# First MLP split into 6 and 10 tiles of features, with every block sum of the second MLP's matrices formed beside the second half and kept in DRAM

## The chip, the cores and the metric

The kernel runs on one core of one Trainium2 chip. The metric is the device time of one execution in microseconds (us); lower is better. Engines are named as the profile names them: PE (TensorE matmuls) and PEld (its weight loads), DVE (VectorE), ACT (ScalarE), POOL (GpSimd), SP (SyncE, which issues the DMAs).

## The reference

Attention over 4 batches, 8 heads, 576 positions and 64 dimensions per head, with a causal mask and a decay bias; then two MLPs over the 2304 tokens of width 512:

```python
x = attn(q, k, v, s)                    # (2304, 512)
h = x @ w_in                            # 512 -> 2048
g = s * relu(h) ** 2 + b
x = g @ w_out                           # 2048 -> 512
h = max(x @ w1, x @ w2, x @ w3)         # 512 -> 768
out = h @ w_fin                         # 768 -> 512
```

The matrices of both MLPs arrive as 64-bit numbers. `w_in` and `w_out` are the first MLP's (inputs `moe_`), `w1`, `w2`, `w3` and `w_fin` the second's (inputs `moe2_`).

## The kernel before

Every MLP product is made from two 32-bit parts of each operand, hi and lo, by three matmuls (`mm3`, lines 252 to 254). A 64-bit matrix is turned into hi and lo on the chip: `weight_steps` (line 266) loads a piece, then runs some nine operations on ACT, DVE and POOL (lines 282 to 297).

The 2048 features of the first MLP are 16 tiles of 128. The first `f_split` = 8 of them (**half A**, matrices `wa_in`, `wa_out`, tiles `g`, `ga`) are worked beside attention: for each of 4 batches and each of 2 parts of its tokens (320 and 256 columns) the products go up to 8 tiles (lines 252 to 254 with `xhi`, `xlo`, `wa_in`), are squared after a relu on DVE and ACT, and come down into 4 tiles of outputs (`ga`, `wa_out`), which wait in DRAM as `y0_d`. Attention itself is 20 jobs, 4 and 4 for the two parts of batch 0 and 12 whole ones; its last product is `px` (line 623). The other 8 tiles (**half B**, `wb_in`, `wb_out`, tiles `gbh`, `gbl`) run after attention and after half A, over 5 groups of tokens (`AT`: two of 384 columns, three of 512). `mlp1` (line 995) records both halves. The matrices of half B are converted during attention in pieces of 256 columns (`side`, line 897; tiles `wb`, `wbs`) and saved in DRAM (`wb_d`), and are loaded when attention's memory is given back (`begin_2`, line 914).

The second MLP's three products use a scheme with 7 products per block of 2 by 2 (Strassen-Winograd), so each matrix is first turned into 7 block sums per half of its rows (a **quad**; `convert_quad`, line 1204; 6 quads in all). Each quad loads four blocks of 128x384 (tiles `wst`, `bl`), runs bit operations on ACT and DVE, and forms hi and lo of seven sums. Three quads (`STAGED`, line 1274) are formed beside the last part of half A, in tiles `sd` that lie where `wb_out` will come, and saved to DRAM (`s_d`); the other three beside half B. The two of `w1` (i = 0) stay in SBUF as `sw`; those of `w2`, `w3` are saved, and loaded piece by piece into 12 slots `sdp` when the third part needs them (`load_s`, line 1371; `weight`, line 1377). `middle_o` (line 922) gives the memory of `sd` to `wb_out`, `middle_2` (line 926) gives half A's memory to half B, and `begin_3y`, `begin_3z`, `begin_3` (lines 941 to 968) give half B's to the second MLP.

The order of the work is not written out by hand. Each step is added with its engines, a cost, a priority, what it needs and which slot of a ring it takes; `Plan.order` (line 96) places all steps one after the other by these costs and so fixes each engine's order for good. Half A's matmuls have the lowest priority on PE and fill what attention leaves. The order on an engine is followed as it stands: an instruction that waits holds up all behind it.

Of the kernel before, what the change touches and what calls it, by code (L numbers as in the profile page):

```python
# [18 lines left out]
P = 128  # L19
# [180 lines left out]
def fused_kernel(ctx, tc, q, k, v, s, w_in, w_out, ms, mb, w1, w2, w3, w_fin, out,  # L200
                 f_split=8):
# [457 lines left out]
    def in_us(fixed, each):  # L659
# [8 lines left out]
                 "ws": 2, "wg": 3, "wx": 1, "wb": 3, "p": 3, "ph": 4, "raw": 2, "hs": 2, "wst": ST2, "bl": 8, "ts": 2, "sp": 12, "s2": 7, "o": 3, "sd": sum(SD), "xs": XS_BUFS, "y0": 3, "g2": 2})  # L668
# [228 lines left out]
    side = pieces(None, NE, NB * P, w_in[:, NA * P:], 512) + pieces(None, NB, DM, w_out[NA * P:, :], 512)  # L897
    for y, piece in enumerate(side):
        for h in range(2):
            z = 2 * y + h  # L900
            t = WB_1 + z * WB_S
            convert("s", z, SidePiece(z, piece.src[piece.c * P:(piece.c + 1) * P, piece.n0 + h * HB:piece.n0 + (h + 1) * HB]), stage_b, [t + d for d in W_AT],
                    [("w", "a", x, 8) for x in WX] + [("av", 2 * NP - 1 - x, g) for x in range(2) for g in jobs[2 * NP - 1].groups], "wb", None, att=True)
            add(("save", z), "SP", (1, 2 * HB), t + 3.5, [("w", "s", z, 8)], save_b, z, att=True)
# [9 lines left out]
    def begin_2():  # L914
# [26 lines left out]
    def begin_3y():  # L941
# [615 lines left out]
```

## Time and profile before

| | |
|---|---|
| time, median of 3 runs | 906.7 us (903.11 to 907.07) |
| the profiled execution's own time | 906.37 us |
| its span, first to last instruction | 904.6 us |
| PE busy | 881.3 us, 97% of the span |
| PEld, DVE, ACT, POOL busy | 89%, 69%, 55%, 37% |
| attention's last product (`px`) | ends at 344.4 us |
| half A's last matmul | 432.5 us |
| mean granted TensorE clock | 0.992 |

The stages follow one another on PE: attention with half A as filler up to 344.4 us, the rest of half A up to 432.5 us, half B, and the second MLP from about 640 us to the end. A matmul's busy time in the profile is longer than the distance at which matmuls follow one another, so distances are read from starts.

### The profile page before, as it was taken

What the parts mean: (1) busy time and instruction counts of PE and PEld (TensorE: products, weight loads), DVE (VectorE), ACT (ScalarE), POOL (GpSimd) and SP (SyncE); (2) the same over time, 40 slices, a digit from 0 to 9 for tenths busy, and PEclk for the clock granted to TensorE, in tenths of its full rate; (3) what the DMA queues carried; (4) which work ended last, traced back from release to release, by engine and by line L of the source; (5) the groups of instructions that cost most, each with busy time, mean ns of one, the idle gap of its engine ahead of it and who ended that gap; (6) DMA issues with size and microseconds to landing.
All of it is one profiled execution on the core that took longest, in us unless ns stands there. A gap on an engine that the chain in (4) does not pass through costs nothing.

```text
span 904.6 us, 16566 instructions
## 1 busy us (share of the span) xinstructions
PE 881.3 (97%) x5598; PEld 804.7 (89%) x5598; DVE 625.8 (69%) x1506; ACT 494.0 (55%) x1241; POOL 334.9 (37%) x359
## 2 busy tenths in 40 slices
PE   7799899999999999999999999999999999999998
PEld 7567798899898899999999888888999899989996
DVE  7799978778778635888349796676666566656660
ACT  4688689999995763455435445254224422532321
POOL 3335447745655322333312333042224422432220
PEclk9899999999999999999999999999999999999999
DMA  7445455675565204686836454438797255715501
GB/s 225 153 136 182 158 171 185 190 231 174 165 217 188 82 21 149 227 282 219 300 126 232 142 180 157 143 107 226 219 286 221 85 163 172 224 71 163 164 24 70
DMA packets 145652, 154.47 MB, mean 171 GB/s; under 512 B 10144, under 2 KB 112288, under 8 KB 145568
## 3 DMA queue, kind: packets, MB, share of 16 engines
q1 hardware_dynamic: 145472, 153.26, 54.2%
q8 instruction: 45, 0.74, 0.3%
q14 instruction: 39, 0.32, 0.1%
q10 hardware_dynamic: 96, 0.15, 0.0%
HBM read 111.36 MB, written 42.01 MB: 170 GB/s over the span
## 4 chain that ended last, share of the span: by engine, by line
PE 62%; DVE 1%; DMA 1%; issue 0%; ACT 0%; SPq 0%; POOL 0%; ACTq 0%; DVEq 0%; POOLq 0%
PE mm L253 20%; PE mm L254 20%; PE mm L252 20%; DMA wst<-in_moe_w_dram 1%; PE px L623 1%; PE pt L604 0%; DVE g L1022 0%; PE ps L546 0%; DVE ya L1084 0%; DVE sd L1153 0%; DVE wst L1180 0%; PE pr L594 0%; ACT bl L1169 0%; DVE bl L1153 0%; DVE wst L1178 0%
## 5 line engine op out<-in xcount | busy, mean ns | idle before, releaser
L1026 ACT ACTIVATE g<-g 128x320 f32<-128x320 f32 (+3 forms) x104 | 51.7, 497 | 93.0 <-DVE g L1022 92.7
L248 POOL TENSOR_TENSOR gbl<-g,gbh 128x512 fp32r<-128x512 f32 (+1 forms) x40 | 50.4, 1261 | 125.6 <-ACT gbh L241 124.7
L563 ACT ACTIVATE pp<-pp,mn 128x192 f32<-128x192 f32 (+4 forms) x160 | 88.6, 558 | 3.6 <-DVE mn L557 3.5
L248 POOL TENSOR_TENSOR ga<-g,ga 128x320 fp32r<-128x320 f32 (+1 forms) x64 | 57.4, 898 | 83.4 <-ACT ga L241 80.7
L248 POOL TENSOR_TENSOR set<-raw,set 64x1152 fp32r<-64x1152 f32 x24 | 64.5, 2687 | 62.7 <-ACT set L480 49.5
L604 PE MATMUL pt<-ident,pp 128*128 128x128 f32 x480 | 78.9, 279 | 7.5 <-ACT pt L241 4.5
L1022 DVE TENSOR_SCALAR g<-mm 128x320 f32<-128x320 f32 (+3 forms) x104 | 54.2, 521 | 44.5 <-PE mm L254 44.0
L252 PE MATMUL mm<-ty,sdp 128*128 128x384 f32 x252 | 84.2, 334 | 0.0
L253 PE MATMUL mm<-ty,sdp 128*128 128x384 f32 x252 | 84.2, 334 | 0.0
L254 PE MATMUL mm<-ty,sdp 128*128 128x384 f32 x252 | 84.2, 334 | 0.0
L252 PE MATMUL mm<-xhi,wa_in 128*128 128x320 f32 (+1 forms) x256 | 79.6, 311 | 1.3 <-DVE ya L1084 1.3
L252 PE MATMUL mm<-ga,wa_out 128*128 128x320 f32 (+2 forms) x256 | 80.3, 314 | 0.1
L254 PE MATMUL mm<-ga,wa_out 128*128 128x320 f32 (+2 forms) x256 | 76.6, 299 | 2.7 <-DVE wa_out L297 2.7
L241 ACT ACTIVATE pt<-pt 128x256 f32<-128x256 f32 (+3 forms) x181 | 72.2, 427 | 11.9 <-PE pt L604 9.0
L253 PE MATMUL mm<-ga,wa_out 128*128 128x320 f32 (+2 forms) x256 | 76.4, 299 | 1.2 <-POOL ga L248 1.2
L253 PE MATMUL mm<-xlo,wa_in 128*128 128x320 f32 (+1 forms) x256 | 75.7, 296 | 0.2 <-POOL xlo L248 0.2
L254 PE MATMUL mm<-xhi,wa_in 128*128 128x320 f32 (+1 forms) x256 | 75.7, 296 | 0.0
L557 DVE CUSTOM_DVE_ANT_0 pp<-late_keys,ps 64x64 f32<-64x64 f32 (+4 forms) x160 | 63.1, 419 | 17.5 <-PE ps L546 10.9
L604 PEld LDWEIGHTS pt<-ident,pp 128*128 128x128 f32 x480 | 56.0, 141 | 16.3 <-ACT pt L241 6.5
L254 PE MATMUL mm<-gbh,wb_out 128*128 128x512 f32 (+2 forms) x160 | 58.9, 368 | 0.0
L252 PE MATMUL mm<-gbh,wb_out 128*128 128x512 f32 (+2 forms) x160 | 58.9, 368 | 0.0
L253 PE MATMUL mm<-gbl,wb_out 128*128 128x512 f32 (+2 forms) x160 | 58.9, 368 | 0.0
(243 smaller groups left out, 2583.6 us busy)
## 6 DMA issues: line engine op xcount, KB each, us to landing
sdp<-s_d SPq DMA_DIRECT2D x126, 256.0 KB, 4.5
wst<-in_moe_w_dram SPq DMA_DIRECT2D x24, 384.0 KB, 5.5
s_d<-sd SPq DMA_DIRECT2D x21, 384.0 KB, 2.5
raw<-in_q_dram SPq DMA_DIRECT2D x24, 288.0 KB, 3.6
raw<-in_k_dram SPq DMA_DIRECT2D x24, 288.0 KB, 3.2
wb_d<-wbs SPq DMA_DIRECT2D x21, 256.0 KB, 2.7
bl<-y_d SPq DMA_DIRECT2D x24, 192.0 KB, 4.4
out_dram<-o SPq DMA_DIRECT2D x18, 256.0 KB, 2.0
```

The lines of the kernel that those rows point to most:

```text
L241: nc.scalar.activation(dst, src, AF.Copy, scale=1.0 if scale is None else scale)
L248: ENGINES[on].tensor_tensor(dst, a, b, op=ALU.subtract)
L252: nc.tensor.matmul(ps, lhs[0], rhs[0], start=first, stop=False)
L253: nc.tensor.matmul(ps, lhs[0], rhs[1], start=False, stop=False)
L254: nc.tensor.matmul(ps, lhs[1], rhs[0], start=False, stop=last)
L557: nc.vector.tensor_tensor_reduce(out=pp[j][i][:n, k0:k1], in0=late_keys[:n, a:a + k1 - k0], in1=ps_.pop((job.n, u, j))[:n, :k1 - k0], scal ...
L563: nc.scalar.activation(p[:n, :w], p[:n, :w], AF.Exp, bias=mns[job.n, j][:n, i:i + 1], scale=-1.0, accum_out=sums[job.n % 2][:n, j, i:i + 1])
L604: nc.tensor.transpose(pt[:, c - c0, :], pp[j][i][:, c * P:(c + 1) * P], ident)
L623: nc.tensor.matmul(px_[job.n][hf][j * D:(j + 1) * D, a0 - h0:h1 - h0], vn[job.n % 2][:, c, j, :], columns(job, pr["p", job.n, j], c, c + 1 ...
L1022: nc.vector.tensor_scalar(st["g", f], st["u", f][:, :n], 0.0, None, op0=ALU.max)
L1026: nc.scalar.activation(st["g", f], st["g", f], AF.Square)
```

## The change

`f_split` becomes 6: half A has 6 tiles of features and half B has 10. The pieces of `w_in` for half A are 384 columns wide in place of 512 (8 pieces, as before), those of `w_out` are 6 in place of 8. Half B's matrices are 40 pieces of 256 columns in place of 32. No quad is formed beside half A any more: `STAGED`, `window` and `middle_o` are gone, all six quads are formed beside half B (in order w3, w3, w2, w2, w1, w1), all are saved to DRAM, and `wb_out` is loaded straight into its tiles. The block sums of `w1` are loaded back into three tiles `sw0`, `sw1`, `sw2` (`load_w`), each 7 loads.

```diff
-WO = ((0, 1, 2), (3, 4, 5), (6, 7))
-SD = (4, 4, 2)
-PACE_S = 3
-F_AT = 10
-F_PACE = 3
+WO = ((0, 1, 2), (3, 4, 5), (6, 7, 8, 9))
+PACE_0 = 0
+PACE_S = 1.6
+F_AT = 15
+F_PACE = 2.4
...
-                 f_split=8):
+                 f_split=6):
...
-    all_a = pieces(lambda: wa_in, NE, NA * P, w_in[:, :NA * P], 512) + pieces(lambda: wa_out, NA, DM, w_out[:NA * P, :], 512)
+    all_a = pieces(lambda: wa_in, NE, NA * P, w_in[:, :NA * P], NA * P // 2) + pieces(lambda: wa_out, NA, DM, w_out[:NA * P, :], 512)
...
-    def middle_o():
-        tiles = [late["rwo"].tile([P, 2, len(fs), DM], F32R, name=f"wb_out{z}", tag=f"wo{z}") for z, fs in enumerate(WO)]
-        late["wb_out"] = {f: tiles[z][:, :, y] for z, fs in enumerate(WO) for y, f in enumerate(fs)}
...
     marks = [k for k in users_a if k[0] in ("mm1", "downa") and (k[:3] == ("downa", 2, 0) or k[1:3] in ((2, 1), (3, 0), (3, 1)))]
-    for z in range(len(side)):
-        add(("w", "b", z, 8), "SP", (1, 1024), FILL + (1000 + 10 * 11 + z if z < len(side) // 2 else 10 * z), ([("begin_2",), ("after", marks[int((0.3 + 0.06 * z) * len(marks))])] if z < len(side) // 2 else [("middle_o",)]) + [("save", 2 * z + h) for h in range(2)], load_b, z)
+    for z in range(NW):
+        add(("w", "b", z, 8), "SP", (1 if z < WHOLE or z >= NI else 2, 1024), FILL + 1110 + z, [("begin_2",), ("after", marks[int((0.25 + 0.035 * z) * len(marks))])] + [("save", 2 * z + h) for h in range(2)], load_b, z)
...
-        ring = "sd" if (i, kk) in STAGED else "s2" if i else None
+        ring = "s2"
...
     def save_s(q, x):
-        nc.sync.dma_start(s_d[q[0] - 1][x][:, 2 * q[1]:2 * q[1] + 2], sds[q, x].bitcast(F32))
+        nc.sync.dma_start(s_d[q[0]][x][:, 2 * q[1]:2 * q[1] + 2], sds[q, x].bitcast(F32))
...
-            return [("middle_2",), up_at(5 + int((4 * y + x) * PACE_S))]
+            return [("middle_2",), up_at(PACE_0 + int((4 * y + x) * PACE_S))]
...
-    STAGED = ((2, 0), (2, 1), (1, 0))
-    for y, (i, kk) in enumerate(STAGED):
-        convert_quad(y, i, (w1, w2, w3)[i], kk, window(y))
-    for y, (i, kk) in enumerate(((1, 1), (0, 0), (0, 1))):
-        convert_quad(3 + y, i, (w1, w2, w3)[i], kk, stage_b_(y))
+    for y, (i, kk) in enumerate(((2, 0), (2, 1), (1, 0), (1, 1), (0, 0), (0, 1))):
+        convert_quad(y, i, (w1, w2, w3)[i], kk, stage_b_(y))
...
+    def load_w(p, x):
+        nc.sync.dma_start(late["sw"][p][:, x].bitcast(F32), s_d[0][x][:, :, p * P:(p + 1) * P])
...
+        if w == g == 0:
+            for x in ORDER:
+                add(("lw", p, x), "SP", (1, 4 * P), next_prio(FIRST), [("begin_3" if p else "begin_3y",)] + ([("after", ("pr0", 0, 3 * p - 2, x))] if p else [("after", ("t", 0, 1, "load", 3))]) + [("save_s", 0, kk, x) for kk in range(2)], load_w, p, x, delay=0.5)
```

What the planner makes of it stands in the orders. Attention's matmuls are the same 80 groups in the same sequence; half A's matmuls are 1152 in place of 1536. Ahead of attention's last `px` stand 672 of them in place of 882; ahead of the last `px` of the ninth job (the first of the 12 whole ones) 126 in place of 174.

The first place is ACT near the start, where the first pieces of `w_in` are scaled after their loads (line 282) and the first transposed probabilities are copied (`pt`, line 241). Before:

```order
L282 ACTIVATE wg<-wg 128x512 x2
L563 ACTIVATE pp_2_161,sums_148<-pp_2_161,mn 128x320
L282 ACTIVATE stage<-stage 128x512 x2
L241 ACTIVATE wa_in<-wg 128x512
L282 ACTIVATE stage<-wst 128x512
L282 ACTIVATE wg<-wg 128x512
L241 ACTIVATE wa_in<-wg 128x512
L241 ACTIVATE wa_in<-stage 128x512 x2
L241 ACTIVATE pt<-pt 128x64 x2
```

Now:

```order
L282 ACTIVATE wg<-wg 128x384 x2
L563 ACTIVATE pp_2_165,sums_152<-pp_2_165,mn 128x320
L282 ACTIVATE stage<-stage 128x384 x2
L241 ACTIVATE wa_in<-wg 128x384
L282 ACTIVATE stage<-wst 128x384
L282 ACTIVATE wg<-wg 128x384
L241 ACTIVATE wa_in<-wg 128x384
L241 ACTIVATE wa_in<-stage 128x384 x2
L241 ACTIVATE pt<-pt 128x64 x2
```

The sequence is the same and only the widths differ; with one more load ahead of these rows, the first copy of `pt` stands behind seven loaded pieces in both.

The second place is DVE where the last pieces of `wa_out` are finished (line 297 writes the lo part), near the eighth job of attention. Before:

```order
L297 TENSOR_TENSOR wa_out<-stage,wst 128x512
L285 TENSOR_SCALAR stage<-stage 128x512 x2
L287 SCALAR_TENSOR_TENSOR stage<-stage 128x512 x2
L245 CAST wa_out<-stage 128x512
L291 TENSOR_SCALAR stage<-stage 128x512 x2
L293 SCALAR_TENSOR_TENSOR stage<-stage 128x512 x2
L248 TENSOR_TENSOR stage<-stage,wa_out 128x512 x2
L297 TENSOR_TENSOR wa_out<-stage 128x512 x2
L285 TENSOR_SCALAR wb<-wb 128x256
```

Now:

```order
L248 TENSOR_TENSOR stage<-stage,wa_out 128x512
L628 TENSOR_TENSOR x_1444<-px,rb 128x256
L297 TENSOR_TENSOR wa_out<-stage,wst 128x512
L245 COPY pt<-pt 128x4x128
L557 ISA pp_4_162,mn<-late_keys,ps,mn 128x288
L557 ISA mn 128x1
L557 ISA pp_0_163,mn<-late_keys,ps 64x64
L557 ISA mn 64x1
L557 ISA pp_1_164,mn<-late_keys,ps 128x192
```

The block of twelve operations on the last two pieces, which stood between the eighth job's last row and the next job's, is gone: `wa_out` ends with its sixth piece, and attention's rows follow at once. On PE the first product with the fifth and the sixth piece of `wa_out` now stands behind all of the next job's score products.

The third place is SP where half B's last group goes down and the second MLP begins (`bl` are blocks of the first MLP's result, `y_d` its stores, `sw` the new tiles, `sdp` the slots):

```order
L1323 DMA bl<-y_d 128x384 x8
L1372 DMA sw_7573<-s_d_0_182 128x4x128
L1372 DMA sw_7573<-s_d_1_183 128x4x128
L1372 DMA sw_7573<-s_d_5_187 128x4x128
L986 DMA y_d<-y_1_5556 128x512
L1372 DMA sw_7573<-s_d_4_186 128x4x128
L1372 DMA sw_7573<-s_d_6_188 128x4x128
L986 DMA y_d<-y_2_5557 128x512
L1372 DMA sw_7573<-s_d_3_185 128x4x128
L1372 DMA sw_7573<-s_d_2_184 128x4x128
L1369 DMA sdp<-s_d_0_189 128x4x128
```

Before, the loads into `sdp` followed the blocks here; now seven loads of `w1`'s sums stand between, and two stores of the last group's first outputs stand among them.

## Rows read from the trace of the kernel before

**Rows 1.** The page's busy times, and the shares of the chain that ended last.

```profile
PE 881.3 (97%) x5598; PEld 804.7 (89%) x5598; DVE 625.8 (69%) x1506; ACT 494.0 (55%) x1241; POOL 334.9 (37%) x359
...
PE 62%; DVE 1%; DMA 1%; issue 0%; ACT 0%; SPq 0%; POOL 0%; ACTq 0%; DVEq 0%; POOLq 0%
```

**Rows 2.** Busy time by stretch: stretch, length, PE, PEld, DVE, ACT, POOL, PEclk, DMA share, GB/s.

```profile
0.00:40.00 40.00, 31.01 (x214) 25.94 (x214) 29.67 (x88) 21.73 (x60) 14.57 (x39) 0.91 0.59 173
40.00:127.70 87.70, 83.25 (x604) 67.61 (x602) 80.39 (x219) 71.17 (x195) 38.43 (x47) 0.96 0.52 164
127.70:344.40 216.70, 212.21 (x1716) 192.96 (x1712) 155.83 (x532) 184.84 (x541) 116.28 (x119) 1.00 0.52 163
344.40:423.00 78.60, 77.31 (x581) 76.32 (x576) 62.60 (x124) 34.75 (x79) 22.26 (x25) 1.00 0.68 229
423.00:632.00 209.00, 209.00 (x1051) 186.51 (x1052) 141.79 (x279) 94.72 (x192) 60.93 (x55) 1.00 0.56 179
```

**Rows 3.** Timeline of PE: 256-column matmuls, 34 steps apart; 512-column ones, 45 steps.

```profile
361.83 0.28 PE L252 MATMUL mm<-xhi,wa_in 128*128 128x256 f32 x1
...
365.91 0.28 PE L253 MATMUL mm<-xlo,wa_in 128*128 128x256 f32 x1
...
509.78 0.39 PE L252 MATMUL mm<-xb,wb_in 128*128 128x512 f32 x1
...
519.98 0.39 PE L252 MATMUL mm<-xb,wb_in 128*128 128x512 f32 x1
```

**Rows 4.** Timeline of ACT and PE near 25 us, with idle time and its releaser.

```profile
22.24 0.69 ACT L282 ACTIVATE stage<-wst 128x512 f32<-128x512 f32 x1 [2.31 <-DMA wst<-in_moe_w_in_dram]
...
25.95 0.66 ACT L282 ACTIVATE wg<-wg 128x512 f32<-128x512 f32 x1 [3.01 <-DMA wg<-in_moe_w_in_dram]
...
28.33 1.54 PE L604 MATMUL pt<-ident,pp 128*128 128x128 f32 x6 [4.07 <-ACT pt L241]
```

**Rows 5.** The stretches around it, in the columns of rows 2.

```profile
20.00:25.00 5.00, 4.26 (x40) 4.02 (x37) 5.00 (x12) 0.69 (x1) 0.00 (x0) 1.00 1.00 290
25.00:30.00 5.00, 1.67 (x8) 1.35 (x10) 1.63 (x3) 3.57 (x10) 1.05 (x1) 0.74 0.36 116
30.00:40.00 10.00, 9.77 (x64) 6.61 (x64) 7.73 (x31) 6.70 (x26) 4.81 (x4) 0.79 0.22 52
```

**Rows 6.** Timeline of DVE and PE near 108 us: last `wa_out` pieces, and who waits.

```profile
108.04 1.29 DVE L297 TENSOR_TENSOR wa_out<-stage 128x512 fp32r<-128x512 f32 x2
...
108.78 0.42 PE L254 MATMUL mm<-ga,wa_out 128*128 128x320 f32 x1 [2.68 <-DVE wa_out L297]
```

**Rows 7.** The stretches around it, in the columns of rows 2.

```profile
105.00:110.00 5.00, 2.32 (x14) 1.82 (x12) 5.00 (x13) 1.94 (x6) 0.00 (x0) 0.94 0.30 110
110.00:116.00 6.00, 6.00 (x26) 5.91 (x25) 5.14 (x15) 3.71 (x10) 3.32 (x2) 0.50 0.10 33
```

**Rows 8.** Side conversions up to 345 us, tiles `wb`, then `wbs`: DVE, ACT, clock, DMA.

```profile
0.00:345.00 345.00, 26.94 (x67) 9.06 (x21) 0.98 0.53 164
...
0.00:345.00 345.00, 56.77 (x128) 16.95 (x40) 0.98 0.53 164
```

**Rows 9.** Groups of instructions, two of half A's on ACT and DVE.

```profile
L1022 DVE TENSOR_SCALAR g<-mm 128x320 f32<-128x320 f32 x32 | 15.6, 486 | 12.0 <-PE mm L254 11.9
...
L241 ACT ACTIVATE ga<-g 128x320 fp32r<-128x320 f32 x32 | 14.9, 467 | 0.5
```

**Rows 10.** The middle of attention, in the columns of rows 2.

```profile
120.00:240.00 120.00, 118.94 (x968) 106.53 (x967) 93.88 (x339) 114.79 (x342) 73.30 (x74) 1.00 0.63 195
```

**Rows 11.** Timeline of POOL and DVE at 85 us.

```profile
84.68 2.64 POOL L248 TENSOR_TENSOR set<-raw,set 64x1152 fp32r<-64x1152 f32 x1
...
84.87 3.02 DVE L287 SCALAR_TENSOR_TENSOR stage<-stage 128x512 int32<-128x512 int32 x1
```

**Rows 12.** DMA issues from the page: count, KB each, us from issue to landing.

```profile
sdp<-s_d SPq DMA_DIRECT2D x126, 256.0 KB, 4.5
```

More of the change, by code (lines that the diff above doesn't have):

```diff
@@ L852, in stage_a @@
                 if ring == "wx":
-                    made["a"] = stages[0][:, 3 * n // 2:2 * n]
+                    made["a"] = stages[0][:, 3 * DM:3 * DM + n // 2]
                     return atp.tile([P, n], F32, name="wst", tag="wx")
@@ L895, in save_b @@
         nc.sync.dma_start(wb_d[z // 2][:, :, z % 2 * HB:(z % 2 + 1) * HB], t)
[L897 to L904, printed above, removed]
+    WHOLE = NB // 4 * NE
+    halves_in = [(c, n0 + h * HB) for n0 in range(0, NB // 4 * 512, 512) for c in range(NE) for h in range(2)] + [(c, n0) for n0 in range(NB // 4 * 512, NB * P, HB) for c in range(NE)]
+    side = [w_in[c * P:(c + 1) * P, NA * P + n:NA * P + n + HB] for c, n in halves_in] + [w_out[(NA + f) * P:(NA + f + 1) * P, h * HB:(h + 1) * HB] for f in range(NB) for h in range(2)]
+    NI, NW = len(halves_in) // 2, len(side) // 2
+    for z, src in enumerate(side):
+        t = WB_1 + z * WB_S
+        convert("s", z, SidePiece(z, src), stage_b, [t + d for d in W_AT],
+                [("w", "a", x, 8) for x in WX] + [("av", 2 * NP - 1 - x, g) for x in range(2) for g in jobs[2 * NP - 1].groups], "wb", None, att=True)
+        add(("save", z), "SP", (1, 2 * HB), t + 3.5, [("w", "s", z, 8)], save_b, z, att=True)
     late = {}
@@ L917, in begin_2 @@
         rwo = open_pool("rwo", stacks["w_out"], 1, "right")
-        late["sd"] = [t[:, y] for z, m in enumerate(SD) for t in (rwo.tile([P, m, 2, HALF], F32R, name=f"sd{z}", tag=f"wo{z}"),) for y in range(m)]
+        tiles = [rwo.tile([P, 2, len(fs), DM], F32R, name=f"wb_out{z}", tag=f"wo{z}") for z, fs in enumerate(WO)]
+        late["wb_out"] = {f: tiles[z][:, :, y] for z, fs in enumerate(WO) for y, f in enumerate(fs)}
         late["xb"] = open_pool("xb", stacks["x"], 1, "right").tile([P, (2 * NE + XS_BUFS) * G1], F32R, name="xb")
         late["wb_in"] = weight_tiles(open_pool("rwi", stacks["w_in"], 1, "right"), "wb_in", NE, NB * P)
-    def middle_o():
-        tiles = [late["rwo"].tile([P, 2, len(fs), DM], F32R, name=f"wb_out{z}", tag=f"wo{z}") for z, fs in enumerate(WO)]
-        late["wb_out"] = {f: tiles[z][:, :, y] for z, fs in enumerate(WO) for y, f in enumerate(fs)}
     def middle_2():
@@ L928, in middle_2 @@
         w3p = open_pool("w3p", ctx, 1)
-        late["sw"] = w3p.tile([P, 7, 2, 2, HALF], F32R, name="sw")
+        late["sw"] = {}
         late["sdp"] = w3p.tile([P, 8 * 2 * HALF], F32R, name="sdp")
@@ L945, in begin_3y @@
         late["ty"] = y3.tile([P, 2, 7, 2, WIDE], F32R, name="ty")
+        late["sw"][0] = y3.tile([P, 7, 4, P], F32R, name="sw0")
         wf[F_ORDER[0]] = y3.tile([P, 2, DM], F32R, name=f"wf{F_ORDER[0]}")
@@ L974, in begin_3 @@
             hs[f] = [p3.tile([P, 2 * WIDE], F32R, name=f"h{z}{f}") for z in range(2)]
+        for p in range(1, PAIRS):
+            late["sw"][p] = p3.tile([P, 7, 4, P], F32R, name=f"sw{p}")
         for f in F_ORDER[4:]:
@@ L1148, in fused_kernel @@
     ORDER = (A11, A12, S2, S1, S3, A22, S4)
-    s_d = [[dram.tile([P, 4, HALF], F32, name=f"s_d{i}_{x}") for x in range(7)] for i in range(2)]
+    s_d = [[dram.tile([P, 4, HALF], F32, name=f"s_d{i}_{x}") for x in range(7)] for i in range(3)]
     blocks, tss, wsts, sds = {}, {}, {}, {}
@@ L1223, in d @@
         def d(hl, x):
-            if not ring:
-                return late["sw"][:, x, hl, kk, :]
             if (q, x) not in sds:
@@ L1239, in split @@
         def split(x, src, needs):
-            seven("q", HALF, x, src, d, pr_, needs + ([] if ring == "sd" else [("middle_2",)]), q, take=[(ring, [("save_s", *q, x)])] if ring else ())
-            if ring:
-                add(("save_s", *q, x), "SP", (1, 2 * HALF), pr_(), done(x), save_s, q, x)
+            seven("q", HALF, x, src, d, pr_, needs + [("middle_2",)], q, take=[(ring, [("save_s", *q, x)])])
+            add(("save_s", *q, x), "SP", (1, 2 * HALF), pr_(), done(x), save_s, q, x)
         split(A11, blk(0), whole(0))
```

26 lines of the change are left out of this document (13 added, 13 removed).

## Prediction, made before the changed kernel ran

> **What bounds the kernel now.** I read the page's busy times first: PE is busy for 97% of the span, no other engine for more than 69% of it [rows 1] (PEld, at 89%, overlaps PE). The chain that ended last is a PE chain; other engines and DMA have a few per cent of it [rows 1]. So a gain must come from PE having less to do, or from PE waiting less. Second, the busy times by stretch [rows 2] show where it waits: 9.0 us of the first 40, 4.5 in the next 87.7, 4.5 in the 216.7 us of whole attention jobs, 1.3 in the rest of half A, and none in half B. Third, the timeline names the two largest waits [rows 4, 6], and the windows around them show what the clock did [rows 5, 7]. What the reader is to see: half B and the second MLP are as dense as they can be, and what can be won lies ahead of 130 us.
>
> The sum is made against the profiled execution, 906.37 us with a span of 904.6, so 1.8 us lie around the span; it is 0.3 us under the median of 906.7. About 0.5% of it (4.5 us) can be told from no change.
>
> **Part by part.**
>
> *Fewer, longer matmuls.* Starts give the distance between matmuls: 4.08 us over 34 steps is 0.120 us for 256 columns, 10.20 over 45 is 0.227 for 512 [rows 3]. The difference, 0.107 us for 256 columns, leaves 13 ns that don't depend on the width; 320 columns come to 0.147 and 384 to 0.173. A tile of features costs 12 matmuls up and 12 down per block of tokens. In half A that is 24 x 4 x (0.147 + 0.120) = 25.6 us, in half B 24 x (2 x 0.173 + 3 x 0.227) = 24.6 us. Two tiles move: 51.2 us go, 49.3 come, 384 matmuls go and 240 come. **-1.9 us**, all of it on PE's path.
>
> The Trainium skill ("TensorE: Matmul & The Clock Gate", Wait — 56ns, not 53.3ns?) puts the fixed part of a matmul at full clock at about 2.5 ns. By that, 144 fewer matmuls would give an estimated 0.4 us and the sum would be 1.5 us smaller; the trace has 13 ns for these matmuls, and I take the trace.
>
> *The start.* ACT copies the first transposed probabilities only after seven pieces of `w_in` have been loaded and scaled (first place in the order). The sixth and the seventh of these loads hold ACT for 2.31 and 3.01 us, and PE, out of warm-up work, waits 4.07 us for that copy [rows 4]. The DMA engines are full just before, at 290 GB/s [rows 5]. A piece shrinks from 512 to 384 columns, by 0.13 MB; seven by 0.92 MB, 3.2 us at that rate. PE's wait falls to about 0.9 us: **-3.2 us**. Bounds: nothing, if another load is late; 6.6 us, if the half clock that followed (2.6 us of it up to 30 us and 4.2 up to 40, from shares of 0.74 and 0.79 [rows 5]) goes as well, half of those 6.8 us. I take the wait alone, since PE has little work there for a faster clock to speed up.
>
> *The last pieces of `wa_out`.* The seventh and eighth pieces end on DVE at about 109.3 us, and PE waits 2.68 us for them [rows 6]. The granted clock is then 0.50 for 6.0 us and 0.94 in the 5 us before [rows 7]: 3.0 + 0.3 us lost. These pieces don't exist any more; the sixth ends ahead of them, and PE asks for the fifth and sixth only behind the next job's scores (second place). So both go: **-6.0 us**. Bounds: nothing, if the wait moves to another piece; 6.0.
>
> *Whole attention jobs.* In this stretch 384 + 324 = 708 of half A's matmuls are now done on PE, counted from the weights they read, `wa_in` and `wa_out`; of the change's 672 ahead of the last `px`, 126 lie before the stretch, so 546 lie in it. 162 fewer at a mean of 0.133 us shorten it by 21.6 us, to 195.1; that work is in the first term already. But ACT and DVE must then do theirs in less time. Eight more side conversions cost 8 x 2.62 us on DVE and 8 x 0.81 on ACT (83.7 and 26.0 us for 32 [rows 8]), if all fall here. 162/24 = 6.75 tiles of features fewer save some 0.45 us on DVE and twice that on ACT each [rows 9]: 3.0 and 6.1 us. DVE comes to 155.8 + 20.9 - 3.0 = 173.7 us, 89% of 195.1; ACT to 184.8 + 6.5 - 6.1 = 185.2, 95%. From 120 to 240 us the trace shows ACT at 95.7% with PE at 99.1%, but DVE at 78.2% only [rows 10]; from 40 to 127.7 DVE is at 91.7% with PE at 94.9% [rows 2]. So it should fit, with a few more waits: **+2.5 us**, between -4.5 (every wait of the stretch gone) and +26.9 (DVE at 78.2%: 173.7 / 0.782 = 222.0). I stay near the low end because PE was at 95 to 99% at both of these loads.
>
> *Three quads move to half B.* DVE's work in half B is 141.8 us of 209 [rows 2]. At most all 62.6 us that DVE does in the rest of half A moves there, and 2 x 5 relus of some 0.7 us: 211 of 258 us, 82%. In the rest of half A DVE stood at 80% and PE waited for 1.3 us of 78.6 [rows 2]. So I cost it at nothing, PE's matmuls being the cover; if the cover fails it is that 1.7% again, 4 us of 258. The rest of half A loses this DVE load; its 1.3 us may go.
>
> *The sums of `w1` through DRAM.* 14 more saves, and 21 loads of 256 KB (4.5 us to landing [rows 12]). The first seven stand on SP behind eight loads of blocks and with two stores among them (third place). These stores wait for the last group's first two outputs, half way down its 120 products, 27.2 us at 0.227; four loads then have 13.6 us to issue and land in, and the first of them is asked for 3 us later still. Twelve loads into `sdp` queue behind, and are asked for one unit (42 x 0.173 = 7.3 us) later. I cost it at nothing; 8 us if it fails (7 x 0.26 MB at the 229 GB/s of rows 2).
>
> **Sum:** -1.9 - 3.2 - 6.0 + 2.5 = -8.6. Span 896.0, time 897.8 us.
>
> **The rivals.**
>
> *The waits come back elsewhere.* PE waits where the next late thing is: the first jobs have little to fill PE with, and DVE, at 91.7% from 40 to 127.7 us [rows 2], gets later pieces no earlier. Then only -1.9 us is left: 904.5 us. For it: 9.0 us of idle PE in the first 40, of which I explain 4.07. Against it: the order puts attention's rows where the two pieces stood.
>
> *VectorE becomes the bound of the whole jobs.* The eight conversions bring DVE operations with two operands from SBUF into a shorter stretch beside POOL. At 85 us such an operation took 3.02 us beside a POOL operation of 2.64 us and ended just after it [rows 11]. If DVE gets no further than 80%, the stretch takes 217.1 us in place of 195.1, 19.5 us more than I forecast: 917.3 us, slower. It decides below about 82% (173.7 / 0.82 = 211.8 us, 14.2 more than forecast, 912.0). For it: 78.2% beside a full ACT [rows 10]. Against it: 91.7% earlier.
>
> The Trainium skill ("SBUF — State Buffer", Who interferes with whom) says that DVE and GpSimd share a pair of ports under an exclusive lock, so that one blocks the other for a whole instruction. By that rule the trace agrees at 85 us, and this rival is what it would come to here.
>
> *The sums of `w1` come late* at the start of the second MLP: 8 us, 905.8 us. Against it: 13.6 us of cover.
>
> **How the numbers follow.** Forecast 0.60, waits elsewhere 0.24, VectorE 0.11, late sums 0.05. The forecast's own range goes from 889 (all bounds of the gains, and the stretch's waits partly gone) to 902. The range of 889 to 910 takes in the second and fourth case and the forecast with a worse third stretch; it leaves out the VectorE case and some of each edge. Faster: the forecast, 0.60. Same: the second and fourth, 0.29. Slower: 0.11.
>
> **What would show it.** Right: PE's wait near 28 us under 1.5 us; no wait on `wa_out` and a clock of 1.00 around 100 us; the last `px` at about 310 us (344.4 - 6.4 for the 48 matmuls that leave the time before the whole jobs - 9.2 - 21.6 + 2.5); PE at 95% or more from the ninth job on, DVE near 89%; no idle PE in half B and at its end. Wrong: PE waiting over 10 us in the whole jobs, with DVE or POOL as the releaser; a wait of the first product with `sw0` on a DMA.

## The result, and the profile after

The changed kernel takes **894.93 us** (median of 4 runs, 893.21 to 895.95) against 905.12 us of the kernel before in the same comparison (4 runs): a ratio of **0.9886, interval 0.9852 to 0.9919**, or 10.3 us faster (7.3 to 13.4). The forecast was 897.8 us, range 889 to 910, from a sum of -8.6 us. The profiled execution of after took 893.21 us with a span of 891.2, 13.4 us less than that of before; that one was 1.2 us above its median, this one is 1.7 below.

The page's busy times and the chain of after, which answer to [rows 1]:

```profile
PE 875.3 (98%) x5454; PEld 793.6 (89%) x5454; DVE 622.6 (70%) x1537; ACT 492.9 (55%) x1246; POOL 324.3 (36%) x347
...
PE 84%; DVE 3%; DMA 2%; issue 1%; ACT 1%; SPq 0%; DVEq 0%; ACTq 0%
```

Busy time by stretch of after, in the columns of [rows 2] (stretch, length, PE, PEld, DVE, ACT, POOL, PEclk, DMA share, GB/s). The cuts are again at 40 us, the ninth job's last `px`, the last `px`, half A's last matmul and the second MLP's first:

```profile
0.00:40.00 40.00, 34.79 (x260) 29.24 (x262) 33.76 (x111) 25.93 (x83) 15.62 (x44) 0.91 0.64 190
40.00:110.00 70.00, 67.37 (x510) 52.99 (x508) 59.87 (x175) 60.83 (x165) 31.04 (x38) 1.00 0.52 157
110.00:305.90 195.90, 192.16 (x1549) 171.92 (x1545) 158.71 (x550) 178.55 (x534) 109.40 (x110) 0.99 0.61 190
305.90:370.00 64.10, 63.71 (x491) 63.35 (x488) 27.35 (x64) 22.39 (x53) 16.68 (x21) 1.00 0.75 251
370.00:616.90 246.90, 246.90 (x1202) 218.80 (x1202) 186.64 (x373) 117.91 (x237) 69.21 (x60) 1.00 0.62 207
616.90:891.20 274.30, 270.37 (x1459) 257.25 (x1457) 156.25 (x267) 87.25 (x179) 82.32 (x76) 1.00 0.59 170
```

What to see: the whole jobs take 195.9 us, where 195.1 + 2.5 was forecast, but DVE does 158.7 us of work in them, not 173.7. Half B has no idle PE although DVE does 186.6 us there. The stretches around the two old waits, same columns, with [rows 5, 7] as their answers before:

```profile
20.00:25.00 5.00, 5.00 (x48) 5.00 (x47) 4.73 (x12) 3.10 (x9) 1.20 (x1) 1.00 0.84 262
25.00:30.00 5.00, 4.80 (x45) 3.58 (x43) 3.57 (x15) 3.21 (x13) 2.12 (x1) 1.00 0.17 39
30.00:40.00 10.00, 9.42 (x78) 6.65 (x78) 9.77 (x39) 9.61 (x38) 3.61 (x8) 1.00 0.68 205
...
105.00:110.00 5.00, 5.00 (x47) 3.70 (x47) 3.99 (x13) 4.90 (x18) 2.43 (x5) 1.00 0.44 110
110.00:116.00 6.00, 6.00 (x52) 5.85 (x49) 3.42 (x14) 5.92 (x20) 4.61 (x4) 1.00 0.70 200
```

Both waits and both spells of half clock are gone. The timeline of ACT and PE at the start, which answers to [rows 4]:

```profile
14.56 10.73 PE L510 MATMUL warm<-ident 128*128 128x128 f32 x80
...
19.94 0.58 ACT L282 ACTIVATE stage<-wst 128x384 f32<-128x384 f32 x1 [1.38 <-DMA wst<-in_moe_w_in_dram]
...
22.03 0.59 ACT L282 ACTIVATE wg<-wg 128x384 f32<-128x384 f32 x1 [1.52 <-DMA wg<-in_moe_w_in_dram]
...
23.75 0.88 ACT L241 ACTIVATE pt<-pt 128x64 f32<-128x64 f32 x4
...
25.13 0.82 PE L604 MATMUL pt<-ident,pp 128*128 128x128 f32 x6
```

The sixth and seventh loads now hold ACT for 1.38 and 1.52 us (2.31 and 3.01 before), the first copy of `pt` starts at 23.75 us, and PE goes from the last of its 80 warm-up transposes straight into `pt`. What sets the start in this profile is the end of that warm-up, 25.1 us, not the copy. The warm-up takes 10.73 us here, with the granted clock at 0.66 from 10 to 20 us; before it took 8.90 us at 1.00.

**Where the 13.4 us of span came from.** Job ends are the last `px` of a job; half A's matmuls ahead of each are counted in the two traces and priced at 0.147 us (0.133 in the whole jobs and behind them).

| stretch | before | after | net of the half A work moved |
|---|---|---|---|
| to the end of job 8 | 99.4 us, 99 matmuls | 93.4 us, 87 | -4.2 |
| job 9 (first whole one) | 28.3 us, 75 | 16.6 us, 39 | -6.4 |
| jobs 10 to 20 | 216.7 us, 708 | 195.9 us, 546 | +0.8 |
| rest of half A | 88.1 us, 654 | 64.1 us, 480 | -0.9 |
| half B | 197.5 us | 246.8 us | 0.0 against the forecast +49.3 |
| second MLP | 274.5 us | 274.3 us | -0.2 |

So 10.6 of the 13.4 us lie ahead of the ninth job's end. The 384 matmuls that left half A come to 51.7 us at these prices against 49.3 that half B grew by; these 2.4 us are most of the rest.

### The profile page after: what moved, and what is told of

The parts are those of the page before. It is cut to its first block, busy times and chain, and to the rows that moved or that the text cites. A ratio compares the mean times of both kernels' runs of the same rounds, so it can differ in the third digit from the quotient of the medians.

```text
span 891.2 us, 16405 instructions
## 1 busy us (share of the span) xinstructions
PE 875.3 (98%) x5454; PEld 793.6 (89%) x5454; DVE 622.6 (70%) x1537; ACT 492.9 (55%) x1246; POOL 324.3 (36%) x347
## 4 chain that ended last, share of the span: by engine, by line
PE 84%; DVE 3%; DMA 2%; issue 1%; ACT 1%; SPq 0%; DVEq 0%; ACTq 0%
PE mm L252 24%; PE mm L254 24%; PE mm L253 24%; PE pt L604 4%; PE px L623 4%; PE ps L546 3%; DVE pp L557 1%; PE pr L594 1%; DMA wb_d<-wb 0%; DMA x_d<-x 0%; DMA set<-dm_d 0%; DMA wbs<-in_moe_w_out_dram 0%; DMA wbs<-in_moe_w_in_dram 0%; DMA wb<-in_moe_w_out_dram 0%; DVE rs L570 0%
## 5 line engine op out<-in xcount | busy, mean ns | idle before, releaser
L1027 ACT ACTIVATE g<-g 128x512 f32<-128x512 f32 (+3 forms) x98 | 50.7, 517 | 90.2 <-DVE g L1023 89.7
L563 ACT ACTIVATE pp<-pp,mn 128x576 f32<-128x576 f32 (+4 forms) x160 | 89.0, 560 | 2.1 <-DVE mn L557 1.9
L252 PE MATMUL mm<-ty,sdp 128*128 128x384 f32 x252 | 84.2, 334 | 0.0
L253 PE MATMUL mm<-ty,sdp 128*128 128x384 f32 x252 | 84.2, 334 | 0.0
L254 PE MATMUL mm<-ty,sdp 128*128 128x384 f32 x252 | 84.2, 334 | 0.0
L1023 DVE TENSOR_SCALAR g<-mm 128x512 f32<-128x512 f32 (+3 forms) x98 | 53.4, 546 | 37.3 <-PE mm L254 31.8
L254 PE MATMUL mm<-gbh,wb_out 128*128 128x512 f32 (+2 forms) x200 | 73.6, 368 | 0.0
L252 PE MATMUL mm<-gbh,wb_out 128*128 128x512 f32 (+2 forms) x200 | 73.6, 368 | 0.0
L253 PE MATMUL mm<-gbl,wb_out 128*128 128x512 f32 (+2 forms) x200 | 73.6, 368 | 0.0
L254 PE MATMUL mm<-xb,wb_in 128*128 128x512 f32 (+1 forms) x200 | 73.4, 367 | 0.0
L252 PE MATMUL mm<-xb,wb_in 128*128 128x512 f32 (+1 forms) x200 | 73.4, 367 | 0.0
L248 POOL TENSOR_TENSOR ga<-g,ga 128x320 fp32r<-128x320 f32 (+1 forms) x48 | 40.8, 851 | 63.2 <-ACT ga L241 61.9
L253 PE MATMUL mm<-xb,wb_in 128*128 128x512 f32 (+1 forms) x170 | 61.8, 363 | 0.0
L252 PE MATMUL mm<-xhi,wa_in 128*128 128x320 f32 (+1 forms) x192 | 60.8, 317 | 0.4 <-DVE ya L1085 0.4
L252 PE MATMUL mm<-ga,wa_out 128*128 128x320 f32 (+2 forms) x192 | 59.7, 311 | 0.0
L546 PE MATMUL ps<-set 128*128 128x288 f32 (+4 forms) x288 | 57.2, 312 | 0.7 <-DMA set<-dm_d 0.3
```

What stands on the lines that cost most here:

```text
L248: ENGINES[on].tensor_tensor(dst, a, b, op=ALU.subtract)
L252: nc.tensor.matmul(ps, lhs[0], rhs[0], start=first, stop=False)
L253: nc.tensor.matmul(ps, lhs[0], rhs[1], start=False, stop=False)
L254: nc.tensor.matmul(ps, lhs[1], rhs[0], start=False, stop=last)
L546: nc.tensor.matmul(ps[:, :k1 - k0], t[:, a, QS[i]:QS[i] + P], t[:, b, k0:k1], start=x == 0, stop=x == 1)
L563: nc.scalar.activation(p[:n, :w], p[:n, :w], AF.Exp, bias=mns[job.n, j][:n, i:i + 1], scale=-1.0, accum_out=sums[job.n % 2][:n, j, i:i + 1])
```

## The experiments

Ratios are to the kernel before, timed beside each run. "Above after" is the ratio less 0.9886, times 905 us; these carry the intervals of both ratios, some 3 to 4 us together. Some added lines shift the line numbers of a kernel by 1 or 3.

**1. The moved quads alone.** The old split with the new placing of the quads:

```diff
-                 f_split=6):
+                 f_split=8):
```

(and `WO` for 8 tiles; all else as in the changed kernel.)

> The kernel before with the second half of the change alone: all six quads formed beside half B and the sums of w1 kept in DRAM, but the first MLP still in 8 and 8 tiles. Theory (the gain is at the start and at the last pieces of wa_out): both of those stay as they were, PE still waits about 4 us near 28 us and about 2.7 us near 108 us; the rest of half A may lose its 1.3 us of waits; time 0 to 2 us below the kernel before. Rival (moving the quads is what gains): at least 6 us below.

Measured: 907.22 us, ratio 1.0024 (1.0002 to 1.0047), 2.2 us slower. The rival is out: the gain is not here. But the theory's "0 to 2 below" missed too. The rest of half A got 2.4 us shorter, half B 1.2 longer (198.7 us) and the second MLP 4.0 longer (278.5 us). Two groups of PE's waits in this kernel (in all, times, longest):

```profile
PE mm L254 <- DVE wa_out L297: 2.7, 1, 2.7
...
PE mm L252 <- DMA sdp<-s_d: 2.4, 1, 2.4
```

The second of them in PE's timeline:

```profile
671.26 0.33 PE L253 MATMUL mm<-ty,sdp 128*128 128x384 f32 x1
671.43 0.34 PE L254 MATMUL mm<-ty,sdp 128*128 128x384 f32 x1
674.15 0.66 PE L252 MATMUL mm<-ty,sdp 128*128 128x384 f32 x1 [2.38 <-DMA sdp<-s_d]
674.61 0.52 PE L253 MATMUL mm<-ty,sdp 128*128 128x384 f32 x1
674.93 0.52 PE L254 MATMUL mm<-ty,sdp 128*128 128x384 f32 x1
```

The old wait for `wa_out` is where it was, and a new one for block sums from DRAM stands in the second MLP, with matmuls 0.32 us apart behind it in place of 0.17. So the move costs something with an 8 and 8 split. With 6 and 10 tiles half B is 48 us longer, and the same wait is absent. SP's queue stands later against PE here: the last of the first twelve loads into `sdp` was issued 11.1 us after the second MLP's first matmul (640.8 against 629.7), in after 1.4 us (618.3 against 616.9). What holds the queue back was not tested.

**2. Six pieces of `wa_out` in the kernel before.**

```diff
-    all_a = ... + pieces(lambda: wa_out, NA, DM, w_out[:NA * P, :], 512)
+    all_a = ... + pieces(lambda: wa_out, NA, DM, w_out[:NA * P, :], 512)[:6]
-    lambda f: (wa_out[0][:, f], wa_out[1][:, f])
+    lambda f: (wa_out[0][:, f % 6], wa_out[1][:, f % 6])
...
-    lambda f: [("w", "a", 2 * NE + f, 8)]
+    lambda f: [("w", "a", 2 * NE + f % 6, 8)]
```

(The lines are shortened to what differs.)

> The kernel before without the seventh and eighth piece of wa_out: the products of tiles 6 and 7 read the first and second piece instead, so this much of the conversion is left out; the number of matmuls is unchanged. Theory: the wait of 2.68 us near 108 us and the half clock behind it both go, 6.0 us (5 to 7) below the kernel before; the granted clock is 1.00 from 100 to 116 us. Rival (the waits come back at the next late thing): within 1.5 us of the kernel before.

Measured: 897.76 us, ratio 0.9922 (0.9894 to 0.9949), **7.1 us faster** (4.6 to 9.6). The stretches around the old wait in this kernel:

```profile
105.00:110.00 5.00, 5.00 (x38) 4.95 (x38) 4.31 (x18) 4.91 (x17) 4.05 (x3) 1.00 0.53 189
110.00:116.00 6.00, 6.00 (x46) 5.84 (x44) 5.30 (x17) 5.70 (x17) 3.55 (x3) 1.00 0.61 202
```

PE is busy throughout and the clock stays at 1.00, against 2.32 of 5 us and 0.50 in [rows 7]. Job 9 takes 19.7 us in place of 28.3; 21 matmuls fewer of half A lie in it (3.1 us), so 5.5 us net. No wait for `wa_out` is left in this profile.

**3. Fewer bytes at the start of the kernel before.**

```diff
-        nc.sync.dma_start(st.bitcast(I64), src)
+        m = src.shape[1] * 3 // 4 if name == "a" and z < 8 else src.shape[1]
+        if m < src.shape[1] and z in (0, 1, 2, 3, 4, 7):
+            nc.gpsimd.memset(st[:, 2 * m:], 0.0)
+        nc.sync.dma_start(st.bitcast(I64)[:, :m], src[:, :m])
...
```

> The kernel before with 384 of the 512 columns loaded of each of the first 8 pieces of w_in (the other quarter is cleared or stale, so that part of the matrix is left out); the operations on ACT and DVE keep their width of 512. Theory (the bytes ahead of the seventh load hold the first copy of pt): PE's wait near 28 us falls from 4.07 to under 1.5 us, time 3.2 us (up to 6.6) below the kernel before. Rival (another thing, such as the stores of dm_d or ACT's own work, holds the copy): the wait stays above 3 us and the time within 1 us.

Measured: 902.35 us, ratio 0.9968 (0.9945 to 0.9991), 2.9 us faster (0.8 to 5.0). ACT and PE at the start (L285 is the scaling after a load here):

```profile
22.88 0.70 ACT L285 ACTIVATE wg<-wg 128x512 f32<-128x512 f32 x1 [1.50 <-DMA wg<-in_moe_w_in_dram]
...
25.11 0.87 ACT L241 ACTIVATE pt<-pt 128x64 f32<-128x64 f32 x4
26.32 0.82 PE L607 MATMUL pt<-ident,pp 128*128 128x128 f32 x6
```

With ACT's and DVE's operations as wide as before, the load ends ACT's wait 3.1 us earlier and the copy starts at 25.1 us; PE's wait at this place is gone, and the clock from 30 to 40 us is 1.00 where [rows 5] has 0.79. The first job ends at 28.8 us (32.9 before). Not all of the vanished wait is the copy's: PE's warm-up also ended 2.2 us later here (26.5 in place of 24.3), with the granted clock at 0.68 from 10 to 20 us where it was 1.00 before. Nor does the copy come at the same time in every profile. With all bytes it started at 28.07, 28.08 and 26.24 us (the kernel before, experiments 1 and 2), with fewer at 25.11 and 25.20 (experiments 3 and 4). So the bytes hold the copy back, by 1 to 3 us in these profiles.

**4. Both edits.** The two diffs above together.

> Both edits at once in the kernel before: six pieces of wa_out, and 384 columns loaded of the first 8 pieces of w_in. Theory: the two terms add, 9.2 us (7 to 13) below the kernel before, and all that is left to the changed kernel is what fewer matmuls give. Rival (one late thing replaces the other): no more than the larger of the two alone, about 6 us.

Measured: 895.77 us, ratio 0.9909 (0.9874 to 0.9944), 8.2 us faster (5.1 to 11.4): about the sum of the two, 10.0, within what the intervals can tell. Its last `px` ends 10.5 us earlier than before. The kernel before with two late things taken away is thus within 2.1 us of the changed one, and this difference, which also holds the -1.9 us for fewer matmuls, is smaller than the intervals.

**5. Two late pieces put back into the changed kernel.**

```diff
+    all_a += all_a[-2:]
...
-    lambda f: [("w", "a", 2 * NE + f, 8)]
+    lambda f: [("w", "a", 2 * NE + f + (2 if f > 3 else 0), 8)]
```

> The changed kernel with the fifth and sixth piece of wa_out loaded and converted a second time, ahead of their first use as the seventh and eighth pieces were (two more conversions of 128x512). Theory (late pieces of wa_out cost a wait and a half clock): PE waits for wa_out again near 95 to 105 us and the clock falls behind it; 3 to 8 us above the changed kernel, ratio to the kernel before about 0.995 (0.992 to 0.998). Rival (with 6 tiles PE asks for them late enough that two more pieces would hide): within 1.5 us of the changed kernel, ratio below 0.990.

Measured: 897.50 us, ratio 0.9921 (0.9890 to 0.9952), 3.2 us above after, at the low edge of the theory, but the two intervals overlap; what this run shows stands in its trace. PE's timeline where it asks for the last piece:

```profile
99.35 0.42 PE L254 MATMUL mm<-ga,wa_out 128*128 128x320 f32 x1 [3.12 <-DVE wa_out L297]
```

The stretches around it, in the columns of [rows 2]:

```profile
95.00:100.00 5.00, 1.38 (x7) 0.74 (x5) 4.97 (x11) 2.44 (x5) 0.00 (x0) 1.00 0.82 260
100.00:105.00 5.00, 4.17 (x18) 4.09 (x18) 4.16 (x14) 3.73 (x9) 2.97 (x2) 0.50 0.11 37
```

The mechanism came back in full, a wait of 3.12 us and then half clock: job 9 takes 26.6 us in place of 16.6, 8.7 net of nine more matmuls. Jobs 10 to 20 then took 192.2 us, 3.7 less than in after with as many of half A's matmuls; that a long wait of PE lets the other engines get ahead would explain it, but it was not tested.

**6. The bytes put back into the changed kernel.** A copy from DRAM to DRAM ahead of each of the first seven pieces:

```diff
...
+        if name == "a" and z < 7:
+            nc.sync.dma_start(spare[z].bitcast(I64), w_out[z * P:(z + 1) * P, :P])
         nc.sync.dma_start(st.bitcast(I64), src)
```

> The changed kernel with a copy of 0.13 MB from DRAM to DRAM ahead of each of the first seven pieces of w_in, 0.92 MB in all, which is what the narrower pieces no longer load. Theory (these bytes set when the first pt is copied): the first copy moves from 23.8 to 26 us or later, PE waits for it again, 3 us (1 to 6.6) above the changed kernel. Rival (the start was gained by something else, such as shorter operations): the copy moves by under 1 us and the time by under 1 us.

Measured: 897.13 us, ratio 0.9927 (0.9903 to 0.9951), 3.7 us above after, but the two intervals overlap. ACT and PE at the start (L242 is the copy here):

```profile
24.65 0.58 ACT L285 ACTIVATE wg<-wg 128x384 f32<-128x384 f32 x1 [1.22 <-DMA wg<-in_moe_w_in_dram]
...
26.37 1.73 ACT L242 ACTIVATE pt<-pt 128x64 f32<-128x64 f32 x6
...
26.64 0.87 PE L607 MATMUL pt<-ident,pp 128*128 128x128 f32 x6 [0.97 <-ACT pt L242]
```

The copy moved from 23.75 to 26.37 us as expected, and PE waits 0.97 us for it. The first job ends 1.5 us later only: PE's warm-up covers the rest. Another 3.3 us of this profile lie in jobs 10 to 20, where nothing was added and the order is that of after; that part is not explained, and it says how far one profile of that stretch can be trusted.

**7 to 9. More work for DVE in the whole jobs.** The forecast had given DVE 173.7 us there and it came to 158.7. So I added what was missing: one operation of a side conversion, which gives the same values when repeated, done twice, three times, or twice in every second conversion (`times` 2, 3, or 1 and 2 in turn):

```diff
+        for _ in range(times):
+            nc.vector.scalar_tensor_tensor(x, word(I32, 1), -2 ** 31, x, op0=ALU.bitwise_and, op1=ALU.bitwise_or)
```

> The changed kernel with one DVE operation of each side conversion done twice (both operands in SBUF, 0.42 us, 40 times, some 35 of them in the whole jobs: 14.7 us, which brings DVE from 158.7 to about 173.4 us of that stretch, the load that the prediction gave it, 89%). Theory (DVE has room): the stretch grows by at most 2.5 us, ratio below 0.993. Rival (beside POOL DVE gets no further than 82%): 173.4 / 0.82 = 211.5 us, 15 us more, ratio above 1.002.

> The same operation done three times: 29.4 us more in the whole jobs, DVE at about 188 of 195.9 us, 96%. Theory (DVE has room up to about what ACT has, 91 to 95%): some waits, 3 to 8 us above the changed kernel. Rival (no further than 82%): 188 / 0.82 = 229 us, 33 us more.

> The changed kernel with the operation done twice in every second side conversion only, some 7.4 us more of DVE's own time in the whole jobs. Theory (a slope: each operation more is stretched and waited for): about half of the 23 us of the full dose, 9 to 14 us above the changed kernel, ratio 0.999 to 1.004. Rival (a ceiling that is reached at about 85%): under 4 us, ratio below 0.993.

Measured: half a dose 902.17 us, ratio 0.9984 (0.9962 to 1.0006); one dose **917.95 us, ratio 1.0144** (1.0106 to 1.0181); two doses 950.29 us, ratio 1.0507 (1.0472 to 1.0542). Jobs 10 to 20 of these kernels (ninth job's end to last `px`), in the columns of [rows 2]; after's line is the third of the table by stretch above. Half a dose:

```profile
110.00:314.70 204.70, 196.14 (x1549) 174.56 (x1545) 170.87 (x566) 179.31 (x534) 109.86 (x110) 0.97 0.58 182
```

One dose:

```profile
109.10:328.80 219.70, 202.64 (x1547) 179.36 (x1545) 186.28 (x580) 179.84 (x532) 110.64 (x110) 0.95 0.54 168
```

Two doses:

```profile
109.80:360.80 251.00, 211.97 (x1547) 185.91 (x1545) 211.85 (x612) 180.90 (x531) 111.31 (x110) 0.92 0.47 147
```

The theory that DVE has room falls. 16, 30 and 62 operations more (6.7, 12.6 and 26.0 us at 0.42) lengthened the stretch by 8.8, 23.8 and 55.1 us: 0.55, 0.79 and 0.89 us for each. The rivals' prices, 15 us for one dose and 33 for two, were too low as well: timed, these doses cost 23.3 and 56.2 us. Half a dose cost 8.9 us timed, just under the 9 to 14 that were expected for a slope and well above the 4 expected for a ceiling. DVE's share ends at 83 to 85% and no dose gets it higher. That is a limit of this stretch and this order only, since DVE stood at 91.7% from 40 to 127.7 us of the kernel before [rows 2]. No free room shows below it: the half dose costs its own time or somewhat more, as near as a stretch that moved by 3.3 us with nothing added can tell.

Where do 23.8 us come from with 12.6 added? DVE's busy time grew by 27.6, so 15 us are operations that got longer. One of them in the timeline, in the kernel with one dose, and what waits for it:

```profile
288.03 0.42 DVE L298 TENSOR_TENSOR wb<-wb 128x256 fp32r<-128x256 f32 x1
...
288.29 2.64 POOL L248 TENSOR_TENSOR set<-raw,set 64x1152 fp32r<-64x1152 f32 x1 [3.21 <-ACT set L481]
...
288.37 3.65 DVE L288 SCALAR_TENSOR_TENSOR wbs<-wbs 128x256 int32<-128x256 int32 x2
...
292.11 0.42 ACT L241 ACTIVATE wbs<-wbs 128x256 fp32r<-128x256 f32 x1 [3.48 <-DVE wbs L288]
292.43 0.37 ACT L241 ACTIVATE pt<-pt 128x256 f32<-128x256 f32 x1
...
292.85 0.48 PE L605 MATMUL pt<-ident,pp 128*128 128x128 f32 x1 [3.04 <-ACT pt L241]
```

Two operations of 0.42 us take 3.65 us: the first does not end before POOL's `set` does. ACT then waits 3.48 us for them, and its next operation is the copy that PE waits 3.04 us for. In this kernel seven of the conversions' operations last over 1.2 us, all beside such a `set`; in after it is one (2.88 us at 160.6). Operations that read PSUM (`pp`, `mn`, `g`, `ya`) ran beside `set` at their normal length. PE's idle time in the stretch grew from 3.7 to 17.1 us, and the mean clock fell from 0.99 to 0.95: 13.3 us of idle and 10.5 us of longer PE busy time are the 23.8. PE has five waits of over 2 us in this stretch (at 129, 204, 222, 272 and 293 us, 12.4 us together), each ending within 3.2 us after one of the seven long operations does, and the clock falls to 0.50 for 6.8 us at three of them (129, 272 and 293). After has no wait of over 2 us there.

The Trainium skill ("SBUF — State Buffer", Who interferes with whom) says that a DVE instruction with two inputs in SBUF contends with a GpSimd instruction that reads SBUF, and one that has at most one SBUF input outside the two-port modes does not. The trace agrees on the first with the pair above, and on the second with the operations from PSUM. Operations with one input in SBUF were stretched too (`wbs`, line 291 of the changed kernel, 2.75 us at 165.8 us with one dose, in place of 0.29), which by that section of the Trainium skill would mean a two-port mode; no run here shows the mode.

**10. One dose, with the planner told of it.**

```diff
-                 ("DVE", dve(n), (2,), [])
+                 ("DVE", dve(n) * (2 if name == "s" else 1), (2,), [])
```

> The changed kernel with one operation of each side conversion done twice on DVE, as in the run with one operation more, but now the planner is told of its cost and can place the rest around it. Theory (what DVE gets done beside POOL is limited: the added operations are themselves stretched there, so no order helps): still 12 us or more above the changed kernel, ratio to the kernel before above 1.002. Rival (it was the fixed order: instructions of attention stood behind an operation that the plan did not know): under 5 us above the changed kernel, ratio below 0.994.

Measured: 904.84 us, ratio 1.0006 (0.9982 to 1.0031), 10.9 us above after, where the untold dose cost 23.3. The theory's "12 or more" and the rival's "under 5" are both off: about half of the loss was the fixed order, half stays. The stretch of this kernel:

```profile
109.50:318.00 208.50, 196.77 (x1566) 176.59 (x1562) 170.02 (x575) 181.51 (x537) 109.52 (x108) 0.98 0.57 177
```

DVE has 25 operations more here, and the stretch is 12.6 us longer, of which 1.8 are twelve more matmuls of half A: 0.43 us each, about their plain length, in one profile of a stretch that can move by 3 us. Here three of the conversions' operations last over 1.2 us, in place of seven. So an operation that the plan knew cost about what it takes, and one that it didn't know about twice as much.

**11. The planner told of longer side conversions, nothing added.** The costs of the four operations that always run on DVE times 1.3:

> The changed kernel with nothing added, but the planner told that the four operations of a side conversion that always run on DVE take 30% longer (their mean in the trace, not the undisturbed time). If the fixed order loses time to the stretched operations, the 3.7 us of idle PE in the whole jobs shrink and the kernel gains 1 to 3 us; if they are only slack that the order already covers, it is within 1.5 us of the changed kernel.

Measured: 891.05 us, ratio 0.9864 (0.9811 to 0.9918): 2.0 us below after, but the intervals overlap nearly whole. The whole jobs take 194.2 us at a clock of 1.00, and PE's idle time in them is 3.3 us where it was 3.7, so the shrinking that was asked about hardly shows. It is the fastest of all, and not shown to be faster than the changed kernel.

**12. The planner told of slower loads,** twice the cost for half A's pieces:

> The changed kernel with the planner told that the loads of half A's pieces take twice as long, which puts the first copies of pt ahead of the last two loaded pieces on ACT. If ACT's place in line behind those loads still holds the start back, the first job ends 1 to 3 us earlier and the kernel gains as much; if the start now hangs on something else (the scores, DVE), it is within 1.5 us of the changed kernel or slower, since later pieces of w_in come later.

Measured: 895.38 us, ratio 0.9899 (0.9850 to 0.9948), 1.2 us above after: no difference that can be told. In its profile the first copy starts at 24.52 us (23.75 in after), with ACT waiting 3.83 us for DVE ahead of it, PE waits 1.6 us for the copy, and the first job ends at 30.5 us (27.6 in after). Moving the copies ahead in ACT's line did not bring them forward.

## Why the prediction was right, step by step

- *Fewer, longer matmuls, -1.9.* Half B grew by 49.3 us, as worked out. That the whole is -1.9 us is not shown by itself: such a difference is below what the runs can tell. By the rule of the Trainium skill ("TensorE: Matmul & The Clock Gate", Wait — 56ns, not 53.3ns?) the term would be an estimated 0.4 us; the distances in the trace speak for 13 ns, but no timed run here decides between the two.
- *The start, -3.2.* Right in mechanism (experiments 3 and 6) and about right in size: -2.9 us timed alone (0.8 to 5.0), -4.2 in the two profiles. The half clock behind the wait went too, a part that I had left to the bound. PE's wait of 0, below the 0.9 forecast, is luck of this profile: part of the warm-up ran at half clock and it ended after the copy. In the run with one dose, whose order is the same, the warm-up ended at 23.2 us and PE waited 0.94 us, with no half clock behind.
- *The last pieces of `wa_out`, -6.0.* Right: -6.4 net in the two profiles, -7.1 us (4.6 to 9.6) timed alone, and the wait with its half clock came back when two pieces were put back.
- *Whole jobs, +2.5.* The stretch came out at 195.9 us (197.6 forecast), but **the step failed twice, in opposite directions**. "DVE comes to 173.7 us, 89%": it came to 158.7, 81%. The eight more conversions were counted as if all fell here. DVE's share of the conversions in the whole jobs (`wb`, then `wbs`), before:

```profile
127.70:344.40 216.70, 24.77 (x61) 8.22 (x19) 1.00 0.52 163
...
127.70:344.40 216.70, 50.17 (x115) 15.64 (x37) 1.00 0.52 163
```

And after, there and behind the last `px`:

```profile
110.00:305.90 195.90, 29.95 (x66) 9.57 (x23) 0.99 0.61 190
305.90:340.00 34.10, 5.82 (x12) 1.59 (x4) 1.00 0.68 219
...
110.00:305.90 195.90, 54.21 (x139) 18.95 (x45) 0.99 0.61 190
305.90:340.00 34.10, 5.19 (x14) 1.70 (x4) 1.00 0.68 219
```

That is 84.2 us in the stretch against 74.9, 9.2 more in place of 20.9. The eight cost 15.2 us in all, 11.0 us of conversions run behind the last `px` where none did before, and 5.0 us fewer run ahead of the stretch. Half A's relus and squares (tile `g`) save 3.6 us in place of 3.0. "So it should fit, with a few more waits": it would not have. The forecast's conversions were known to the planner, so the nearest run is the dose that it knew (experiment 10): with 170.0 us of DVE the stretch took 208.5, or 206.7 without the twelve matmuls, against 197.6 forecast. With a dose that it did not know the stretch took 219.7. The argument that PE was at 95% with DVE at 91.7% from 40 to 127.7 us was weak from the start: that stretch holds the wait for DVE's last pieces of `wa_out` and its half clock [rows 6, 7]. That the stretch came out near the forecast all the same is luck: two errors of one step cancelled.
- *Three quads to half B, 0, and the sums of `w1`, 0.* Right for the changed kernel: no idle PE in half B, the second MLP as long as before. Experiment 1 points to the longer half B as the cover: with 8 and 8 tiles the same move costs 4.0 us in the second MLP. In the prediction this cover was named for DVE's load only.
- *The rivals.* "Waits come back elsewhere" did not happen (experiments 2 to 4). "VectorE becomes the bound" did not happen but lay close. Its mechanism, DVE operations held up beside POOL, is in the traces. Its price, 217.1 us for the stretch and 917.3 us in all, was reached only by the dose that the order did not know (219.7 and 917.95 us); the dose that the planner knew took the gain away (904.84 us) and no more. A chance of 0.11 was given to it by my estimate of the load, which was too high, and of the room, which was too high as well. The signs I named were PE at 95% or more (98%), the last `px` near 310 us (305.9) and DVE near 89% (81%): the last one is what gave the failed step away.

## What to carry to other kernels

A wait of PE can cost more than its length: both waits that this change removed (4.07 and 2.68 us) had a spell of half clock behind them, where waits of 0.94 and 0.97 us in two of the runs had none. Taking away what came late (bytes ahead of a queue, two conversions ahead of a consumer) removed both. Before moving work onto an engine that runs near 80% beside another that reads SBUF, measure its room by repeating a harmless operation: a share of busy time below 100% is not room, and here each operation added to the whole jobs cost about its own time when the order knew it and up to about twice that when it did not. When a forecast comes true, check its inner numbers too.

## What was not expected of the hardware

- How few collisions carry the price: six more conversions' operations that met a `set` of POOL, some 2.2 us longer each, are 13 of the 15 us by which DVE's operations grew with one dose. In the pair shown the operation started 0.08 us after the `set` did.
- The start of the same order differs from one execution to the next, and with it the wait. In the run with the quads alone, in which ACT's order and the bytes at the start are those of before, the first copy of `pt` started at 28.08 us, as before (28.07). PE waited 2.22 us for it, not 4.07, since its warm-up, partly at half clock, ended at 26.1 us in place of 24.3. Before, then in that run:

```profile
15.36 8.90 PE L510 MATMUL warm<-ident 128*128 128x128 f32 x80
...
10.00:20.00 10.00, 7.76 (x65) 6.65 (x65) 9.87 (x30) 7.57 (x20) 2.38 (x4) 1.00 0.81 269
```

```profile
16.09 10.02 PE L510 MATMUL warm<-ident 128*128 128x128 f32 x80
...
10.00:20.00 10.00, 8.41 (x50) 6.88 (x50) 9.81 (x29) 7.61 (x21) 2.18 (x4) 0.66 0.88 282
```

The clock behind the wait, from 30 to 40 us, was 0.50 there and 0.79 before. A wait of this kind is known from one profile only to some 2 us.
